# The last product of an output projection, its copy and its store in one piece instead of two, and two pairs of output rows stored by one transfer each

## The chip, the cores and the metric

The kernel runs on one core of a Trainium2 chip. The metric is the device time of one execution in microseconds (us); the number compared is the median of several executions. All times of instructions below come from one profiled execution.

## What is computed

Attention with a mask by cluster, and then a gated feed-forward layer. Each query and each key is assigned to the one of 16 centroids of its head that is nearest by angle; a query sees only the keys of its own cluster. The result, laid out as 3072 tokens of 512 features, goes through the feed-forward layer. The change touches the last matrix product alone, `@ w_out`, and the storing of its result.

```python
def _attn_ref(q, k, v, centroids):          # q, k, v: 4 x 8 x 768 x 64; centroids: 8 x 16 x 64
    ...
    mask = q_assign[:, :, :, None] == k_assign[:, :, None, :]
    scores = scale * np.matmul(q, k.transpose(0, 1, 3, 2))
    scores = np.where(mask, scores, -1000000000.0)
    ...
    return np.matmul(attn, v).astype(np.float32)

def _moe_ref(x, w_gate, w_val, w_out):      # x: 3072 x 512; w_gate, w_val: 512 x 1536; w_out: 1536 x 512
    gate = 1.0 / (1.0 + np.exp(-(x @ w_gate)))
    val = x @ w_val
    return (gate * val @ w_out).astype(np.float32)
```

## The kernel before

**Stages.** The four batches run one after another. Of each batch the 768 tokens are cut into six chunks of 128, interleaved: token 6p + c is row p of chunk c. Chunks 0, 2, 4 form the first group of a batch and chunks 1, 3, 5 the second; for the first batch the groups are cut a little differently. For each group the kernel runs attention over four pairs of heads, then `feed` (gate and value products, hidden tile hT), and then `project` for the output rows. TensorE (PE in the profile) works on attention of the next group while the feed-forward layer of the last one is interleaved with it. Only behind the last group of the last batch is there nothing to interleave.

**The output projection.** `project` (line 1292) takes two chunks at a time and forms a 2 x 2 block product (two chunks by the two halves of 256 output columns) with seven products in place of eight. Each product is six matmuls of 128 x 256 (line 1375), accumulated over the hidden features in a bank called ring. The operand sums that this needs are made by VectorE (DVE) in `add` (line 1345), into tiles named s_114, s_115 and s_116 for one pair of chunks, and into pieces of the tiles nat_64 and nat_66 for another pair that is under way at the same time. Results are put together by `halved` (line 1393 on ScalarE, ACT; line 684 where it is done on VectorE) and `summed` (line 1400), into an output tile `out2` (there are two, out20_112 and out21_113 in the program; each holds two rows of 512 columns, one per chunk). The four quarters are called c11, c12 (first chunk) and c21, c22 (second chunk); p4 is the product that ends the block, and c21 is its copy. `project` is a generator, so that for the last group of the last batch (`end`) two pairs of chunks go forward in turns: the first pair writes out_112, the last pair (`final`) writes out_113. In that group each sum of `add` is made in two halves (three hidden chunks each), and the products can begin on the first half.

**The last pair.** For the pair that ends the program, p4 is formed in two halves of 128 columns, each six matmuls of 128 x 128. The first half is copied by ACT, the second by DVE, and each half is stored by itself: the first on the queue of SyncE (SP), the second on the queue of ACT. The second row of the pair before it is also stored on ACT's queue.

**Stores.** All other rows leave by `store` (line 1431), one transfer of 128 x 512 (256 KB) per chunk, on SP's queue. A chunk whose two quarters are done early (c11, c12) is stored before the other.

**Order of the work.** Every instruction is a task. `schedule` (line 230) walks through modelled time and for each engine picks, among the tasks that could start within 0.02 us of the earliest, the one with the lowest place. The places stand in a table of numbers (PLACES), and the modelled landing time of each transfer in another (LANDINGS). Each engine then runs its tasks strictly in the order that comes out. Transfers of the SP and ACT queues take eight completion semaphores in turn, DMAHW0 to DMAHW7; a transfer waits until the eighth before it has landed. At the end of the program (line 1818, or 1822 after the change) SP waits for every one of those semaphores, in the order of their numbers, before the engines meet in a last barrier.

Of the kernel before, what the change touches and what calls it, by code (L numbers as in the profile page):

```python
# [112 lines left out]
"""  # L113

LANDINGS = """
# [12 lines left out]
"""  # L128


# [22 lines left out]
class Order:  # L153
# [76 lines left out]
    def schedule(self):  # L230
# [5 lines left out]
        for t in self.tasks:  # L236
            if not t.todo:
                wait.setdefault(t.eng, []).append(t)
        free = {e: 0.7 for e in {t.eng for t in self.tasks}}
        order, under_way, pool, twin = [], {"SP": [], "POOL": []}, (0.0, 0.0), (0.0, 0.0)  # L240
        while any(wait.values()):
            best = None
            for e, ts in wait.items():
                cand = []
                for t in ts:
                    r = t.ready
                    for tag in {b.tag for b in t.acq}:
                        f = self.free_slots(tag, sum(b.tag == tag for b in t.acq), max(t.ready, free[e]))[0]
                        r = None if f is None or r is None else max(r, f)
                    if r is not None:  # L250
                        r = max(r, free[e])
                        if t.both and r >= pool[0]:
                            r = max(r, pool[1])
                        if e == "POOL" and not t.dma and r >= twin[0]:
                            r = max(r, twin[1])
                        cand.append((r, t))
                if not cand:
                    continue
                first = min(c[0] for c in cand)
                start, t = min(  # L260
                    (c for c in cand if c[0] <= first + 0.02), key=lambda c: (c[1].due, c[0])
                )
                if best is None or start < best[0]:
                    best = (start, t)
            assert best is not None, [(t.eng, t.due, [b.tag for b in t.acq]) for ts in wait.values() for t in ts][:30]
            start, t = best
            wait[t.eng].remove(t)
            now = max(t.ready, free[t.eng])
            free[t.eng] = start + t.dur
            t.start = start  # L270
# [41 lines left out]
def kernel(  # L312
# [12 lines left out]
    B, H, S, D = q.shape  # L325
# [924 lines left out]
    HM = DM // 2  # L1250
# [41 lines left out]
    def project(b, one, two, final, many, end):  # L1292
# [144 lines left out]
        if final:  # L1437
            yield
            store(0, 0, DM, [c11, c12])
            store(1, HM, DM, [c22])  # L1440
            for lo, hi in ((0, HM // 2), (HM // 2, HM)):
                p4 = product(
                    X, False, lambda: a(1, 1), lambda i: views["t4"][:, i], [c22, weighed[-1]], [], [r1, *hs], lo=lo, hi=hi
                )
                c21 = halved(
                    lambda lo=lo, hi=hi: o2.tile[:, 1, lo:hi], lambda lo=lo, hi=hi: X()[:, lo:hi], [p4], [], [r1, o2],
                    "DVE" if lo else "ACT", hi - lo,
                )
                store(1, lo, hi, [c21], "ACT" if lo else "SP")
            h_last[h1] = h_last[h2] = p4  # L1450
            return
        if end:
# [1 line left out]
        p4 = product(X, False, lambda: a(1, 1), lambda i: views["t4"][:, i], [c22, *weighed[-NWG:]], [], [r1, *hs])  # L1454
        c21 = halved(out_part(1, 0), X, [p4], [], [r1, o2])
        h_last[h1] = h_last[h2] = p4
        store(0, 0, DM, [c11, c12])
        store(1, 0, DM, [c21, c22], "ACT" if end else "SP")

    wsums_of = {}  # L1460

# [361 lines left out]
```

## Time and profile before

| | |
|---|---|
| median of 3 runs | 309.78 us (309.48 to 310.14) |
| profiled execution, its own time | 309.38 us |
| span of that execution, first to last instruction | 307.6 us |
| PE busy | 299.2 us, 97% of the span |
| DVE, ACT busy | 249.3 us (81%), 259.0 us (84%) |
| granted TensorE clock | 1.000 of full speed |
| PE's last product ends | about 303.8 us into the span |
| last compute instruction ends (copy of the last half) | about 304.4 us |
| last store lands | about 306.4 us |

The times in the rows are counted from the start of the span. Engine PE is the matmul stream and PEld the loading of its weights, which overlaps it. A row of the timeline gives the start, the time from the first start to the last end of the instructions merged in it, engine, line and operation, and in brackets how long the engine had been idle and whom it waited for. SPq and ACTq are the queues of SP and ACT, which issue transfers. The time of the execution is 1.8 us more than the span.

### The profile page before, as it was taken

To read this page: it belongs to the slowest core of one execution; us is meant where nothing else is said; L and a number is where in the kernel's file an instruction comes from. 1 tells how busy PE (TensorE), PEld (TensorE's weight loads), DVE (VectorE), ACT (ScalarE), POOL (GpSimd) and SP (SyncE) were. 2 spreads that over 40 slices of the span, in tenths; PEclk is the share of its full clock that TensorE was granted. 3 is DMA by queue.
4 is the path that set the end of the run, shared out by engine and by line. 5 is a ranking of instruction groups with operands and counts; after the bars stand their busy time and mean duration, and the time that the engine had idled before them with its cause. 6 is when DMAs were issued, how large, how long until landed. Compare 5 with 4: busy or idle time off the path is not lost.

```text
span 307.6 us, 8905 instructions
## 1 busy us (share of the span) xinstructions
PE 299.2 (97%) x3491; PEld 237.5 (77%) x3491; DVE 249.3 (81%) x604; ACT 259.0 (84%) x449; POOL 79.2 (26%) x112
## 2 busy tenths in 40 slices
PE   7998899999999999999999999999999999999994
PEld 3676588754468688977998779987998889988974
DVE  4999996897886687889789989979778738964993
ACT  4898799884448899999999989999999998995841
POOL 5898849741022033600001301470000000000000
PEclk9999999999999999999999999999999999999999
DMA  6999999994557595931384674893210120131003
GB/s 222 368 287 181 218 202 145 181 137 85 97 90 160 111 128 166 118 47 22 84 134 90 104 119 118 178 124 29 71 37 26 40 61 34 25 74 70 0 3 136
DMA packets 97833, 34.79 MB, mean 113 GB/s; under 512 B 83152, under 2 KB 93568, under 8 KB 97792
## 3 DMA queue, kind: packets, MB, share of 16 engines
q1 hardware_dynamic: 72192, 24.57, 34.6%
q0 software_dynamic: 24880, 8.92, 29.2%
q10 hardware_dynamic: 720, 0.75, 0.7%
q8 instruction: 27, 0.44, 0.6%
q14 instruction: 14, 0.11, 0.1%
HBM read 28.87 MB, written 6.29 MB: 114 GB/s over the span
## 4 chain that ended last, share of the span: by engine, by line
PE 89%; ACT 4%; DVE 3%; DMA 2%; issue 1%; ACTq 0%; SPq 0%
PE ring L1584 25%; PE ring L1114 19%; PE ring L1375 18%; PE ring L1506 11%; PE ring L1165 10%; ACT es L1138 3%; PE ring L794 3%; DMA nat<-in_q_dram 1%; PE ring L902 1%; DVE hT L1631 1%; DMA out<-in_centroids_dram 1%; DVE t L684 1%; PE ring L942 1%; DVE even L681 0%; ACT t L909 0%
## 5 line engine op out<-in xcount | busy, mean ns | idle before, releaser
L1138 ACT ACTIVATE es<-ring,nbias 128x768 f16<-128x768 f32 (+1 forms) x189 | 169.8, 941 | 15.1 <-PE ring L1114 10.5
L1165 PEld LDWEIGHTS <-es 128*128 128x128 f16 x1152 | 51.3, 97 | 11.7 <-ACT es L1138 0.8
L1165 PE MATMUL ring<-vp,es 128*128 128x65 f16 x1152 | 56.6, 193 | 0.0
L757 POOL CAST even<-t 128x768 f16<-128x768 f32 x24 | 21.1, 892 | 116.3 <-issue 37.3
L1615 DVE TENSOR_TENSOR nat<-ring,nat 128x384 f32<-128x384 f32 x68 | 36.7, 552 | 14.9 <-ACT nat L1603 8.6
L1622 ACT ACTIVATE nat<-nat 128x384 f32<-128x384 f32 x68 | 37.3, 575 | 1.9 <-DVE nat L1615 1.9
L1584 PEld LDWEIGHTS <-wss 128*128 128x128 f16 x408 | 34.8, 98 | 2.2 <-issue 0.2
L1603 ACT COPY nat<-ring 128x384 f32<-128x384 f32 x68 | 33.9, 519 | 2.7 <-PE ring L1584 1.7
L1584 PE MATMUL ring<-nat,wv 128*128 128x192 f16 x272 | 32.6, 246 | 0.0
L1584 PE MATMUL ring<-nat,wss 128*128 128x192 f16 x272 | 32.4, 246 | 0.0
L1584 PE MATMUL ring<-x,wg 128*128 128x192 f16 x272 | 32.3, 246 | 0.2 <-DVE hT L1631 0.2
L1375 PEld LDWEIGHTS <-hT 128*128 128x128 f16 x294 | 27.2, 97 | 4.9 <-DVE hT L1631 0.4
L1375 PE MATMUL ring<-wo,hT 128*128 128x256 f16 x216 | 29.0, 272 | 0.1
L1114 PE MATMUL ring<-even 80*128 80x384 f16 (+2 forms) x120 | 26.4, 294 | 0.9 <-ACT es L1138 0.6
L1114 PE MATMUL ring<-even,odd 80*128 80x384 f16 (+2 forms) x120 | 26.8, 293 | 0.0
L1114 PE MATMUL ring<-odd 80*128 80x384 f16 x96 | 26.5, 325 | 0.1
L1114 PE MATMUL ring<-odd,even 80*128 80x384 f16 x96 | 26.4, 326 | 0.2 <-ACT es L1138 0.2
L1584 PEld LDWEIGHTS <-wv 128*128 128x128 f16 x272 | 23.3, 97 | 3.0 <-issue 0.2
L1114 PEld LDWEIGHTS <-even 80*128 80x128 f16 x216 | 19.5, 98 | 7.1 <-issue 3.5
L1114 PEld LDWEIGHTS <-odd 80*128 80x128 f16 x216 | 19.3, 98 | 6.6 <-issue 4.5
L1584 PEld LDWEIGHTS <-wg 128*128 128x128 f16 x272 | 23.1, 98 | 1.5 <-issue 0.4
L1506 PE MATMUL ring<-x,wg 128*128 128x256 f16 (+2 forms) x112 | 22.5, 326 | 0.1
(120 smaller groups left out, 519.0 us busy)
## 6 DMA issues: line engine op xcount, KB each, us to landing
out_dram<-out SPq DMA_DIRECT2D x22, 256.0 KB, 2.4
nat<-in_k_dram SPq DMA_DIRECT2D x32, 96.0 KB, 3.1
nat<-in_q_dram SPq DMA_DIRECT2D x32, 96.0 KB, 3.0
odd<-even SPq DMA_DIRECT2D x12, 192.0 KB, 3.5
vp<-in_v_dram POOLq DMA_DIRECT2D x24, 96.0 KB, 5.2
nat<-in_k_dram SPq DMA_DIRECT2D x5, 384.0 KB, 6.2
nat<-in_q_dram SPq DMA_DIRECT2D x5, 384.0 KB, 5.7
nat<-in_v_dram SPq DMA_DIRECT2D x4, 384.0 KB, 7.2
```

Of the source, the lines that this page charges most:

```text
L684: nc.vector.tensor_scalar(to, of, by, None, ALU.mult)
L757: nc.gpsimd.tensor_copy(t[:, NM[nm], cols], t32[p, nm].tile[:, cols])
L794: nc.tensor.matmul(out=ps[32 * g : 32 * g + 32, half, :QB], lhsT=cblk[:, 2 * p + half, :], rhs=t32[p, nm].tile[:, half * QB : (half + 1) * ...
L1114: nc.tensor.matmul(out=to, lhsT=kb.tile[0:80, 0, e * QB + j // 2 * 128 : e * QB + (j // 2 + 1) * 128], rhs=qb_.tile[0:80, 1, e * QB + c0 * ...
L1138: i = nc.scalar.activation(to, of, AF.Exp, bias=nbias, scale=D ** -0.5 if quarters(b, p) else scale,).ins
L1165: nc.tensor.matmul(out=av.tile[:, g : g + D + 1], lhsT=es.tile[:, i * N + c * 128 : i * N + (c + 1) * 128], rhs=vp[:, e, j, :], start=firs ...
L1375: nc.tensor.matmul(out=ps[:, lo:hi], lhsT=left_()[:, i], rhs=right(i)[:, lo:hi], start=new and i == 0, stop=i == NFC // 2 - 1, skip_group_ ...
L1506: nc.tensor.matmul(out=ps[:, :N], lhsT=ws[fc // FPG][:, dcc, fc % FPG, :], rhs=xb.tile[:, dcc, :N], start=(dcc == 0), stop=(dcc == NDC - 1),)
L1584: nc.tensor.matmul(out=ps[:, f], lhsT=w_[:, d, f], rhs=x_()[:, d], start=new and not (f or d), stop=d == 1, skip_group_check=True,)
L1603: nc.scalar.copy(held(i), bank(r_))
L1615: lambda: nc.vector.tensor_tensor(held(i), bank(r_), held(i), ALU.add), deps,
L1622: lambda: nc.scalar.activation(held(i), held(i), AF.Tanh, scale=0.5), [m], due_ffn(work), lat=0.16,
```

## The change

What was done for the pair that ends the program, in the lines of `project`:

```diff
-            for lo, hi in ((0, HM // 2), (HM // 2, HM)):
-                p4 = product(
-                    X, False, lambda: a(1, 1), lambda i: views["t4"][:, i], [c22, weighed[-1]], [], [r1, *hs], lo=lo, hi=hi
-                )
-                c21 = halved(
-                    lambda lo=lo, hi=hi: o2.tile[:, 1, lo:hi], lambda lo=lo, hi=hi: X()[:, lo:hi], [p4], [], [r1, o2],
-                    "DVE" if lo else "ACT", hi - lo,
-                )
-                store(1, lo, hi, [c21], "ACT" if lo else "SP")
+            p4 = product(X, False, lambda: a(1, 1), lambda i: views["t4"][:, i], [c22, weighed[-1]], [], [r1, *hs])
+            c21 = halved(out_part(1, 0), X, [p4], [], [r1, o2])
+            store(1, 0, HM, [c21], "ACT")
```

So p4 of that pair is one product of six matmuls of 128 x 256, copied by one instruction of ACT and stored by one transfer of 128 x 256 (128 KB) on ACT's queue. For all other pairs:

```diff
+        if b == B - 2 and chunk1 < chunk2:
+            dma(
+                "SP", lambda: out_v[b, chunk1 : chunk2 + 1 : chunk2 - chunk1].rearrange("c p m -> p c m"),
+                lambda: o2.tile, 1.34, [c11, c12, c21, c22], due_ffn(work()), uses=[o2],
+            )
+            return
         store(0, 0, DM, [c11, c12])
-        store(1, 0, DM, [c21, c22], "ACT" if end else "SP")
+        store(1, 0, DM, [c21, c22])
```

In the last but one batch (b = 2) the pairs of chunks (0, 2) and (3, 5) are stored by one transfer of 512 KB each, when all four quarters are there; the pair (4, 1), whose chunks are not in rising order, is stored by two transfers as before. The second row of the first pair of the last group moves from ACT's queue to SP's.

`schedule` now takes, on each engine, only the task with the lowest place among all that are left, so that the places alone set each engine's order:

```diff
+        line = {e: deque() for e in free}
+        for t in sorted(self.tasks, key=lambda t: t.due):
+            line[t.eng].append(t)
...
+                    if t is not line[e][0]:
+                        continue
```

The table of places is renumbered for the fewer tasks, and three entries leave the table of landings; a line of the places:

```diff
-1556 1593 1618 1616 1643 1656 1706 1735 1745 1754 1770 1777 1719 1727 1750 1783 1786 1790 1801 1828 1794 1812 1818
+1556 1593 1618 1616 1643 1656 1706 1735 1745 1754 1770 1777 1719 1727 1750 1783 1785 1788 1800 1827 1793 1811 1817
```

The banks and tiles that each instruction uses are the same as before. On PE only the last product differs. On ACT two instructions move one place each, both in the feed-forward layer of the last group: a copy of a bank (L1603) goes ahead of a tanh (L1622), and a tanh of a gate (L1673) goes ahead of another tanh (L1622).

**VectorE, the operand sums of the last group.** s_114, s_115 and s_116 are the sums of the first pair, nat_64 and nat_66 those of the last pair, out_113 is a quarter of the output. What is in brackets are the semaphores an instruction waits for. Before:

```order
L1345 TENSOR_TENSOR s_114<-hT_109 128x384 [waits DVE_49] x2
L1345 TENSOR_TENSOR s_115<-s_114,hT_108 128x384 [waits DVE_49] x2
L1345 TENSOR_TENSOR nat_64<-hT_109 128x384 x2
L1345 TENSOR_TENSOR nat_64<-nat_64,hT_109 128x384 [waits DVE_49] x2
L1345 TENSOR_TENSOR s_116<-hT_108,s_115 128x384 x2
```

And after:

```order
L1349 TENSOR_TENSOR s_114<-hT_109 128x384 [waits DVE_49] x2
L1349 TENSOR_TENSOR s_115<-s_114,hT_108 128x384 [waits DVE_49]
L1349 TENSOR_TENSOR nat_64<-hT_109 128x384 x2
L1349 TENSOR_TENSOR nat_64<-nat_64,hT_109 128x384 [waits DVE_49]
L1349 TENSOR_TENSOR s_115<-s_114,hT_108 128x384
L1349 TENSOR_TENSOR nat_64<-nat_64,hT_109 128x384 [waits DVE_49]
L1349 TENSOR_TENSOR s_116<-hT_108,s_115 128x384
L1349 TENSOR_TENSOR s_116<-hT_108,s_115 128x384 [waits DVE_49]
```

The second half of s_115 moved behind three instructions of nat_64, which each stand one place earlier.

**ScalarE and SyncE, the end of the program.** Two rows of copies and the stores that follow. The DMAHW semaphore that a store waits for is also the one it will set when it has landed; where none is shown, it is the next in turn. Before, ACT first and then SP:

```order
L1393 ACTIVATE out_112<-ring 128x256 [waits DMAHW1_49,PE_49]
L1393 ACTIVATE out_113<-ring 128x128 [waits DMAHW4_49,DVE_49,PE_49]
L441 DMA out_dram<-out_112 128x512 [waits DMAHW0_49,Activation_49]
L441 DMA out_dram<-out_113 128x128 [waits DMAHW2_49,DVE_49]
L441 DMA out_dram<-out_112 128x512 [waits DMAHW5_49,DVE_49]
L441 DMA out_dram<-out_113 128x512 [waits DMAHW6_49,DVE_49]
L441 DMA out_dram<-out_113 128x256 [waits DMAHW7_49,DVE_49]
L441 DMA out_dram<-out_113 128x128 [waits DMAHW1_49,Activation_49]
```

And after, ACT first and then SP:

```order
L1397 ACTIVATE out_112<-ring 128x256 [waits DMAHW7_49,PE_49]
L1397 ACTIVATE out_113<-ring 128x256 [waits DMAHW2_49,PE_49]
L445 DMA out_dram<-out_113 128x256 [waits Activation_49]
L445 DMA out_dram<-out_112 128x512 [waits DMAHW3_49,DVE_49]
L445 DMA out_dram<-out_113 128x512 [waits DMAHW4_49,DVE_49]
L445 DMA out_dram<-out_113 128x256 [waits DMAHW5_49,DVE_49]
L445 DMA out_dram<-out_112 128x512 [waits DMAHW6_49,Activation_49]
```

One store less is left, the second row of out_112 stands on SP instead of behind the last copy on ACT, and the last three to land set the semaphores 5, 6 and 7 where they set 0, 1 and 2.

**SyncE, the second merged store of the last but one batch.** x_107 is the input of the last group's feed-forward layer, brought in by transposing transfers. Before:

```order
L1223 DMA_TRANSPOSE x_107<-xn_102 128x3x128 [waits DMAHW6_49,DVE_49,PE_49]
L441 DMA out_dram<-out_112 128x512 [waits DMAHW7_49,DVE_49]
L1223 DMA_TRANSPOSE x_107<-xn_103 128x3x128 [waits DMAHW0_49,DVE_49,PE_49]
L441 DMA out_dram<-out_112 128x512 [waits DMAHW1_49,Activation_49]
L1223 DMA_TRANSPOSE x_107<-xn_104 128x3x128 [waits DMAHW2_49,DVE_49,PE_49]
```

And after:

```order
L1227 DMA_TRANSPOSE x_107<-xn_102 128x3x128 [waits DMAHW5_49,DVE_49,PE_49]
L1227 DMA_TRANSPOSE x_107<-xn_103 128x3x128 [waits DMAHW6_49,DVE_49,PE_49]
L445 DMA out_dram<-out_112 128x2x512 [waits DMAHW7_49,Activation_49]
L1227 DMA_TRANSPOSE x_107<-xn_104 128x3x128 [waits DMAHW0_49,DVE_49,PE_49]
```

The first of the two stores is gone, and the merged one stands where the second one stood.

More of the change, by code (lines that the diff above doesn't have):

```diff
@@ L267, in schedule @@
             wait[t.eng].remove(t)
+            line[t.eng].popleft()
             now = max(t.ready, free[t.eng])
```

74 rows, old and new, of tables (LANDINGS, PLACES) are left out of this document.

## The prediction, made before the changed kernel was run

> **What bounds the kernel now.** I read the page first: the share of each engine, then the chain of work that ended last.
>
> ```profile
> PE 299.2 (97%) x3491; PEld 237.5 (77%) x3491; DVE 249.3 (81%) x604; ACT 259.0 (84%) x449; POOL 79.2 (26%) x112
> PE 89%; ACT 4%; DVE 3%; DMA 2%; issue 1%; ACTq 0%; SPq 0%
> ```
>
> TensorE (PE) sets the time nearly everywhere. An edit elsewhere pays only where PE stands still, or behind PE's last product. So next I read the chain in order of time, for PE's last piece in it, and the timeline of what follows.
>
> ```profile
> 295.84 7.93 PE ring L1375 x75
> ...
> 302.27 1.49 PE L1375 MATMUL ring<-nat,hT 128*128 128x256 f16 x18
> 303.12 0.38 ACT L1393 ACTIVATE out<-ring 128x256 f32<-128x256 f32 x1 [2.25 <-PE ring L1375]
> 303.79 0.28 ACT L1393 ACTIVATE out<-ring 128x128 f32<-128x128 f32 x1 [0.29 <-PE ring L1375]
> 303.85 0.92 ACTq L441 DMA_DIRECT2D out_dram<-out  x2
> 304.10 0.29 DVE L684 TENSOR_SCALAR out<-ring 128x128 f32<-128x128 f32 x1 [1.23 <-ACT out L1393]
> ```
>
> The cut of the last product in two buys nothing here. ACT's copy of the first half starts at 303.79, when both halves are done (302.27 + 1.49 = 303.76), and DVE's copy of the second half waits for ACT. Product, copy, copy: all in a row. The last row's store leaves ACT's queue right after, at about 304.42 (303.85 + 0.92, less the 0.35 that one issue takes).
>
> Then come the stores, and the waits by which SP ends the program (line 1818), in three stretches of time:
>
> ```profile
> L441 ACTq DMA_DIRECT2D out_dram<-out x1: 351/351/351, 304.4 to 304.4; - x1
> out_dram<-out ACTq DMA_DIRECT2D x1, 256.0 KB, 2.1
> out_dram<-out SPq DMA_DIRECT2D x1, 128.0 KB, 1.7
> out_dram<-out SPq DMA_DIRECT2D x1, 64.0 KB, 2.0
> out_dram<-out ACTq DMA_DIRECT2D x1, 64.0 KB, 2.0
> ...
> L1818 SPq EVENT_SEMAPHORE  x3: 28/28/28, 305.9 to 306.4; - x3
> ...
> L1818 SPq EVENT_SEMAPHORE  x5: 28/28/28, 306.5 to 306.7; - x5
> L1818 SPq DRAIN  x1: 7/7/7, 306.8 to 306.8; - x1
> ```
>
> The three waits end when the last three stores land: 303.85 + 2.1, 304.09 + 2.0, 304.42 + 2.0 = 306.4. They are numbers 0, 1 and 2 of the eight completion semaphores. The five that follow are for transfers long landed, and still take about 0.06 each, one after another: 0.3 us between the last landing and the drain at 306.8. From there to the end of the span (307.6) it is a fixed 0.8.
>
> **The change, part by part.** I work from PE's last stall to the barrier, minus being a gain.
>
> *VectorE's new order.* In the last group PE goes through products of six matmuls, 0.66 apart when it doesn't wait:
>
> ```profile
> 296.83 0.82 PE L1375 MATMUL ring<-nat,s 128*128 128x256 f16 x6
> 297.24 0.62 DVE L1345 TENSOR_TENSOR nat<-hT 128x384 f16<-128x384 f16 x2
> 297.64 0.55 PEld L1375 LDWEIGHTS <-nat 128*128 128x128 f16 x6 [0.28 <-DVE nat L1345]
> 297.65 0.83 PE L1375 MATMUL ring<-nat,nat 128*128 128x256 f16 x6
> 297.78 0.62 DVE L1345 TENSOR_TENSOR nat<-nat,hT 128x384 f16<-128x384 f16 x2
> 298.31 0.62 DVE L1345 TENSOR_TENSOR s<-hT,s 128x384 f16<-128x384 f16 x2
> 298.31 0.82 PE L1375 MATMUL ring<-nat,s 128*128 128x256 f16 x6
> 298.97 0.82 PE L1375 MATMUL ring<-wo,s 128*128 128x256 f16 x6
> ```
>
> The product at 297.65 begins 0.82 after the one before it: 0.16 late, for the first sum in nat. With the second half of s_115 put behind, that sum starts one DVE step (0.27, half of 297.78 - 297.24) earlier, at 296.97, and is done by 297.32 (0.35 each), before PE is ready at 297.49. **-0.16.** What is late next? The moved half of s_115 is now done at 298.13; the fourth matmul of its product wants it at about 298.4. s_116 starts at 298.31 as before, and its first half is done at 298.66; its product would now begin at 298.81, with weights loaded a tenth ahead, at 298.70. That margin of 0.04 is the thin place. Bounds: 0 if this wait takes all back, -0.16 if nothing does. I take -0.16, since only a margin has to hold, not a new overlap.
>
> *The last product whole.* Eighteen matmuls lie in the row at 302.27: six of 256 columns, 0.11 apart, then twelve of 128. From the first start to the last it is 1.49 - 0.22 = 1.27, less 0.66 for the six, so 0.056 each for the twelve. Twelve by 0.056 is 0.67, six by 0.11 is 0.66: nothing to win or lose, **-0.01**, bounds -0.05 and +0.05. The Trainium skill (TensorE: Matmul & The Clock Gate, section Back-to-back issue gap) gives some 81 ns as the sustained spacing for 128 columns where weights change each time; by that figure the cut would cost 0.3 us more than the rows show and its end would give that back. The trace disagrees, with its 56 ns.
>
> *One copy for two.* Before: 303.79 to 304.39 (304.10 + 0.29). Now one ACT copy of 128 x 256, 0.38 by the row at 303.12: 303.79 to 304.17. **-0.22**, bounds -0.18 and -0.25 by the few hundredths between instructions.
>
> *The last store.* It was 64 KB, 304.42 to 306.4. Now it is 128 KB on the same queue. The nearest row of that size is SP's, 1.7; the nearest of that queue is ACT's store of 256 KB, 2.1. Why did 64 KB take longer than 128 KB? Three stretches of the DMA view, 304.6 to 305.3, 305.3 to 305.66 and from there to 306.0, tell which queue moved:
>
> ```profile
> q10 hardware_dynamic: 107, 0.22, 85.2%
> ...
> q1 hardware_dynamic: 124, 0.06, 62.2%
> q10 hardware_dynamic: 48, 0.05, 39.4%
> ...
> q10 hardware_dynamic: 133, 0.06, 66.6%
> ```
>
> q10 is ACT's queue, q1 SP's. The store of 256 KB, issued at 303.85, held the engines to about 305.4; the two of 64 KB stood behind it and behind each other. In the new kernel the 256 KB no longer wait behind ACT's last copy: they go out on SP when their own copy is done, at 303.12 + 0.38 = 303.50, and so move to about 305.1 (0.35 earlier). The last store is issued at 304.20 and would begin to move 0.8 later (as 303.85 did at 304.6), at 305.0. So it is held up by a tenth: 1.7 + 0.1 = 1.8 against 2.0. **-0.2**, bounds -0.3 (1.7 alone) and +0.1 (2.1, as ACT's large one).
>
> *The waits at the end.* The last store now sets semaphore 7, the last in the row, so the other seven waits are over when it lands. What stood behind the last landing, five waits of 0.06, falls away: **-0.3**. Bounds -0.3 and 0, the latter if SP's other store landed last. That one is issued 0.7 earlier (303.50 against 304.20) and takes 2.1, so it lands at 305.6 against 306.0.
>
> *The merged stores, the shorter SP queue, the two swaps on ACT.* The merged stores replace 256 KB with 512 KB at the place of the second, and their users are far away:
>
> ```profile
> 229.44 0.35 SPq L441 DMA_DIRECT2D out_dram<-out  x1
> 236.83 1.19 SPq L1223 DMA_TRANSPOSE x<-xn  x1
> ...
> 271.45 0.34 SPq L441 DMA_DIRECT2D out_dram<-out  x1
> 274.23 1.18 SPq L1223 DMA_TRANSPOSE x<-xn  x1
> x<-xn SPq DMA_TRANSPOSE x1, 2.4
> 280.81 1.46 PE L1506 MATMUL ring<-x,wg 128*128 128x384 f16 x8
> DMA to landing us min/median/max: 1.7/2.3/4.1
> ```
>
> Behind the second, at 271.45, SP's next is a transpose, issued 2.8 us later and landed at 276.6; PE reads its tile at 280.8. Another 256 KB hold the engines for some 0.8 (the 256 KB above, 304.6 to 305.4). The cover is 4.2 us. Behind the first, at 229.44, the next transpose comes 7.4 later. **0**, bounds 0 and +0.1. The two issues that go free 0.35 us of SP each, and between these rows SP waits anyway. The ACT swaps exchange neighbours:
>
> ```profile
> 285.69 0.54 ACT L1622 ACTIVATE nat<-nat 128x384 f32<-128x384 f32 x1
> 287.73 0.54 DVE L1631 SCALAR_TENSOR_TENSOR hT<-nat,ring 128x384 f16<-128x384 f32 x1
> 293.17 0.52 ACT L1622 ACTIVATE nat<-nat 128x384 f32<-128x384 f32 x1
> 294.30 0.55 DVE L1631 SCALAR_TENSOR_TENSOR hT<-nat,p 128x384 f16<-128x384 f32 x1
> ```
>
> The tanh at 285.69 goes behind a copy of 0.5; even 0.9 late it is done at 287.1, and its reader on DVE is at 287.73. The one at 293.17 is at worst a neighbour's 0.45 late, done by 294.15, and its reader is at 294.30. **0**; without that cover hT, and PE's first product of the projection, would come up to 0.4 later.
>
> *Sum.* -0.16 - 0.01 - 0.22 - 0.2 - 0.3 = -0.89, say -0.9. The span goes from 307.6 to 306.7, and the profiled execution from 309.38 to 308.5. The median of the runs shown is 309.78, 0.4 above that execution, so against it I expect **308.9**.
>
> **The rivals.** *The last store is no shorter.* It keeps ACT's 2.1: the sum is -0.16 - 0.01 - 0.22 + 0.1 - 0.3 = -0.6, **309.2**. For it: the one large store on that queue took 2.1. Against it: that store has twice the bytes, and the time goes with the bytes where nothing stands ahead (1.7 for 128 KB). The Trainium skill (DMA: Bandwidth & Descriptors, section Anatomy of one DMA, a fit for GpSimd's path) has a constant 2.0 us and the bytes by 436 GB/s on top: 2.3 for 128 KB against 2.15 for 64 KB. By it the larger store would land later and the sum would be an estimated -0.4; the row of 1.7 speaks against it.
>
> *The change takes away a chain, but not its end.* Should SP's waits cost the same wherever the last store stands among them (0.3 lost), and the stall of PE come back at s_116 (0.16 lost), -0.4 is left: **309.4**. For it is only the thin margin at 298.7; against it, the five waits without any work between them.
>
> *Slower: the merged store holds back the last group's input.* Place: the transpose at 274.23 behind the 512 KB. The slowest 256 KB store here took 4.1; were a merged one to take twice that, 8.2, and the transpose to wait for all of it, the tile would land 5.8 (8.2 - 2.4) later, at 282.4, and PE, at 280.8, would stand for 1.6. Less 0.9: +0.7, **310.5**. It decides from a delay of 4.2 on and makes the kernel slower from 5.1. Against it: the engines are held 0.8 by 256 KB, not 4.
>
> **How the numbers follow.** Forecast 0.67, first rival 0.18, second 0.10, slower 0.05. Within 0.2%, 0.62 us, this kernel's measurement can't tell a difference from none. The forecast is beyond it (-0.9, its own bounds some -0.7 to -1.0, so 308.7 to 309.1). The first rival lies at the limit, half on either side. So faster 0.67 + 0.07 = 0.74, the same 0.11 + 0.10 = 0.21, slower 0.05. The range takes in both milder rivals, 309.4 and 0.2 more since the runs before spread by 0.3 about their median, and below the sum with all bounds at their best (-1.05) and the same spread: 308.3 to 309.6.
>
> **What would show it.** In the profile of the changed kernel: no idle time of the weight load before the first nat product at about 297.5; PE's last row ending at about 303.6; one ACT copy of 0.38 behind it and an issue on ACTq right after, near 304.0; 128 KB landed in 1.7 to 1.9; the drain of SP within 0.1 of that landing, near 305.9; a span near 306.7. The forecast is wrong if the last landing is as late as 306.2, if five waits still follow it, or if PE waits anywhere before 296 where it did not.

## The result, and the profile after

| | before | changed | ratio (95% interval) |
|---|---|---|---|
| median, first comparison | 309.95 us, 22 runs | 308.88 us, 22 runs | 0.9974 (0.9961 to 0.9986) |
| median, repeated | 309.91 us, 20 runs | 308.58 us, 5 runs | 0.9953 (0.9934 to 0.9972) |
| profiled execution, its time | 309.38 us | 308.76 us | |
| its span | 307.6 us | 307.0 us | |
| start of PE's last piece in the chain of waits | 295.84 | 296.11 | |
| from there to the last landing | 10.54 | 9.93 | |
| from there to SP's drain | 10.93 | 10.02 | |

The kernel became faster. The medians differ by 1.07 us and, repeated, by 1.33 us; the intervals of the ratio are wider, from 0.4 to 1.2 us and from 0.9 to 2.0 us. The end of the program, read below, gives 0.91 us, 0.3%, which both intervals hold. The prediction was 308.9 us, and -0.89 by its sum. The ratio leaves out one slow execution of the kernel before (314.82 us) and is not the quotient of the two medians. The last two rows are differences of moments in the records of the trace, that is its single events (semaphore updates at 306.38 and 306.05 for the last landings, the drains at 306.77 and 306.13), taken before rounding; the rows quoted below round these moments to a tenth.

The page's line on the engines, of the changed kernel:

```profile
PE 299.4 (98%) x3485; PEld 237.7 (77%) x3485; DVE 249.0 (81%) x603; ACT 259.1 (84%) x449; POOL 78.9 (26%) x112
```

And the end of its chain of waits, in order of time (start, duration, what):

```profile
296.11 7.74 PE ring L1379 x69
303.85 0.02 issue
303.88 0.38 ACT out L1397
```

Nothing changed in kind. PE still sets the time, and behind it stand one copy and one store. The piece of 7.93 has become 7.74, with 69 matmuls for 75. It starts at 296.11, 0.27 later than in the profile of before: that is not in the prediction, and has an experiment of its own below. The timeline of the same stretch:

```profile
297.10 0.82 PE L1379 MATMUL ring<-nat,s 128*128 128x256 f16 x6
297.24 0.62 DVE L1349 TENSOR_TENSOR nat<-hT 128x384 f16<-128x384 f16 x2
297.65 0.64 PEld L1379 LDWEIGHTS <-nat 128*128 128x128 f16 x6
297.76 0.82 PE L1379 MATMUL ring<-nat,nat 128*128 128x256 f16 x6
...
298.41 0.82 PE L1379 MATMUL ring<-nat,s 128*128 128x256 f16 x6
298.59 0.62 DVE L1349 TENSOR_TENSOR s<-hT,s 128x384 f16<-128x384 f16 x2
...
299.07 0.82 PE L1379 MATMUL ring<-wo,s 128*128 128x256 f16 x6
...
302.37 1.47 PE L1379 MATMUL ring<-nat,hT 128*128 128x256 f16 x12
...
303.88 0.38 ACT L1397 ACTIVATE out<-ring 128x256 f32<-128x256 f32 x1 [0.27 <-PE ring L1379]
304.29 0.35 ACTq L445 DMA_DIRECT2D out_dram<-out  x1
```

Two things are to be read here. The product at 297.76 stands 0.66 behind the one at 297.10, where before the change the same two stood 0.82 apart, and the weight load ahead of it has no bracket any more: it waits for nothing. And behind PE's last row (302.37 + 1.47 = 303.84) there is one copy and one issue, where there were two copies and an issue. Then the last stores in the view of the DMA issues (count, size, median us from issue to landing):

```profile
out_dram<-out SPq DMA_DIRECT2D x3, 256.0 KB, 2.1
out_dram<-out SPq DMA_DIRECT2D x1, 128.0 KB, 1.7
out_dram<-out ACTq DMA_DIRECT2D x1, 128.0 KB, 1.8
```

And SP's waits from 305.9 on (duration in ns, first and last start in us):

```profile
L1822 SPq DRAIN  x2: 7/7/7, 306.1 to 306.2; - x2
L1822 SPq EVENT_SEMAPHORE  x1: 28/28/28, 306.1 to 306.1; - x1
```

The last store takes 1.8 (1.76 in the records) in place of 2.0. When it lands, a single wait ends, at 306.1, and the drain follows in the same tenth: the five waits that stood behind the last landing are gone. The second merged store and the transpose behind it, in the view of the DMA issues:

```profile
out_dram<-out SPq DMA_DIRECT2D x1, 512.0 KB, 3.1
...
x<-xn SPq DMA_TRANSPOSE x1, 2.3
```

And both in the timeline, with the product that reads the transposed tile:

```profile
271.71 0.39 SPq L445 DMA_DIRECT2D out_dram<-out  x1
274.50 1.18 SPq L1227 DMA_TRANSPOSE x<-xn  x1
...
281.08 1.46 PE L1510 MATMUL ring<-x,wg 128*128 128x384 f16 x8
```

The 512 KB took 3.1, and the transpose behind them 2.3, against 2.4 before. PE's product starts 0.27 later than before (281.08 against 280.81), which is the lateness that the whole execution has.

### The profile page after: what moved, and what is told of

It is laid out like the page before. It is cut to its first block, busy times and chain, and to the rows that moved or that the text cites. A ratio compares the mean times of both kernels' runs of the same rounds, so it can differ in the third digit from the quotient of the medians.

```text
span 307.0 us, 8884 instructions
## 1 busy us (share of the span) xinstructions
PE 299.4 (98%) x3485; PEld 237.7 (77%) x3485; DVE 249.0 (81%) x603; ACT 259.1 (84%) x449; POOL 78.9 (26%) x112
## 4 chain that ended last, share of the span: by engine, by line
PE 84%; DVE 7%; ACT 5%; issue 2%; DMA 1%; DVEq 0%; ACTq 0%
PE ring L1588 22%; PE ring L1118 18%; PE ring L1379 18%; PE ring L1510 11%; PE ring L1169 10%; PE ring L798 3%; ACT es L1142 3%; DVE hT L1635 1%; ACT nat L1626 1%; DVE even L685 1%; ACT nat L1607 1%; DMA out<-in_centroids_dram 1%; DVE odd L685 1%; DVE t L660 1%; PE ring L906 1%
```

## The experiments

Each kernel is the changed one but for the edit shown. All are read in the same way: from the start of PE's last piece in the chain (expectations call it the start of the hT product) to the last landing, and from there to the drain. That takes out whatever made an execution early or late before. "Turn" is the order in which transfers take the eight completion semaphores. In the edits of e1, e2, e7 and e8 the calls that only give a store its place in its engine's order are left out.

### Two stores again, and the turn alone

e1 puts the two stores of each merged pair back, and the turn moves on by two.

```diff
         if b == B - 2 and chunk1 < chunk2:
-            dma("SP", lambda: out_v[b, chunk1 : chunk2 + 1 : chunk2 - chunk1].rearrange("c p m -> p c m"), ...)
+            store(0, 0, DM, [c11, c12])
+            store(1, 0, DM, [c21, c22])
             return
```

> The changed kernel, but the two pairs of the last but one batch are stored by two transfers each again, as before the change. The turn of the completion semaphores moves on by two, so the second row of the first pair sets semaphore 0 and the last store semaphore 1. My account (the merging itself is worth nothing, its whole effect is that the last store sets semaphore 7): the tail from the start of the last group's hT product to the last landing is as in the changed kernel (296.11 to 306.05, 9.94), and behind the last landing stand six more waits of 0.06, so the drain comes 0.4 to 0.5 after the landing instead of 0.08; span and time +0.37. Rival A (the waits at the end cost the same in any order): drain 0.1 after the landing, +0. Rival B (the merged stores won or lost time themselves, by SP or by the DMA engines, between 229 and 281): products of the last group start earlier or later by more than the 0.3 that the starts of two executions differ by in the first 30 us, or PE waits for x where it did not.

e2 keeps the merged stores and moves the turn by two at the other end of the program (`od.own` holds the tasks whose place stands outside the table; while it is empty, the first pair that fits is taken).

```diff
+        if b == 0 and 2 not in (chunk1 // 2, chunk2 // 2) and not od.own:
+            for which, done in ((0, [c11, c12]), (1, [c21, c22])):
+                store(which, 0, HM, done)
+                store(which, HM, DM, done)
+            return
         store(0, 0, DM, [c11, c12])
         store(1, 0, DM, [c21, c22])
```

> The changed kernel with its merged stores; only two stores of the first batch are cut into two transfers each, far from the end, so that the turn of the semaphores moves on by two: the last store sets semaphore 1 instead of 7. My account: nothing else changes; the last landing stands where it stood (9.94 after the start of the hT product of the last group), the drain 0.4 to 0.5 behind it instead of 0.08, time +0.37. Rival A (order of the waits is free): +0, the drain 0.1 behind the landing. If e1 shows the same as this one, the merging is worth its shift of the turn and no more.

e9 takes the two stores of e1 and cuts all six stores of the first batch, so that the turn comes round to where it was.

> As e1, the pairs of the last but one batch stored by two transfers each; but all six stores of the first batch are cut into two transfers, so that the turn of the semaphores moves on by eight in all and the last store sets semaphore 7 again. My account (of the merging only the turn matters): the drain follows 0.08 behind the last landing, as in the changed kernel, and from the start of the last group's hT product to the drain it takes 10.01, within 0.03; time as the changed kernel, -0.35 against e1. Rival (two stores in place of one cost something of their own, which e1's later start hid): 10.1 or more, or a later start of the last group than any kernel with the same offset at 30 us has.

SP's waits from the last landing on, of e1:

```profile
L1828 SPq EVENT_SEMAPHORE  x7: 28/28/28, 306.2 to 306.5; - x7
L1828 SPq DRAIN  x2: 7/7/7, 306.6 to 306.6; - x2
```

The same of e2:

```profile
L1834 SPq EVENT_SEMAPHORE  x7: 28/28/28, 306.8 to 307.1; - x7
L1834 SPq DRAIN  x2: 7/7/7, 307.2 to 307.3; - x2
```

And of e9:

```profile
L1832 SPq DRAIN  x2: 7/10/13, 306.3 to 306.4; - x2
L1832 SPq EVENT_SEMAPHORE  x1: 28/28/28, 306.2 to 306.2; - x1
```

In e1 the wait that the last store ends is the first of seven, and the drain comes 0.45 behind the landing (306.59 less 306.14). In e9, with the same two stores, it is the last, and the drain comes 0.08 behind. e2, merged but turned, has seven waits from 306.8 to 307.1 and 0.45 again. Up to the last landing e1, e2 and e9 are like the changed kernel (9.93): 9.93, 9.92 and 9.94 from the start of the piece. So the whole worth of the merged stores is their count. They take two of the three transfers out of the turn that the change takes out (the third is the last store's other half), and without these two the end is 0.37 later; cutting early stores in two makes up for them as well. Rival A of e1 and e2 (the order of the waits is free) and rival B (merging wins or loses time of its own) have both fallen.

The times go the same way, but can't show the size: e1 309.38 us, ratio to before 1.0 (0.9985 to 1.0015); e2 309.16 us, 0.9988 (0.9969 to 1.0008); e9 308.89 us, 0.9965 (0.9951 to 0.9978). The end of e1 is 0.55 shorter than that of the kernel before (10.38 for 10.93), which is a little more than the interval of its ratio allows (0.46). Four of its ten executions took over 310.3 us; why is not shown.

### VectorE's order as before

The place of one task, the second half of s_115, is set back ahead of the pieces of nat_64; nothing else.

```diff
+    od.own[od.tasks[2332]] = ("entry", 2341.5)
     od.run()
```

> The changed kernel, but VectorE makes its operand sums of the last group in the order of before: the second half of s_115 ahead of nat_64. My account: the product that reads nat_64 begins 0.82 behind the one before it instead of 0.66, everything behind it moves by 0.16, and from the start of the hT product to the drain it takes 10.17 instead of 10.01; time +0.16. Rival A (the stall is only moved: in the changed kernel PE waits later, for s_116 or a bank, so the order buys nothing): 10.0, +0. Rival B (the order is what made the whole gain, by a bank or a tile that comes free earlier at the end): +0.4 or more.

PE's piece in its chain of waits:

```profile
296.35 7.91 PE ring L1387 x69
```

And in its timeline PE's two products with the weight load between them:

```profile
297.34 0.82 PE L1387 MATMUL ring<-nat,s 128*128 128x256 f16 x6
...
298.15 0.55 PEld L1387 LDWEIGHTS <-nat 128*128 128x128 f16 x6 [0.27 <-DVE nat L1357]
298.15 0.83 PE L1387 MATMUL ring<-nat,nat 128*128 128x256 f16 x6
```

The wait for nat is back (298.15 is 0.81 behind 297.34), and the piece is 7.91 against 7.74, with the same 69 matmuls: +0.17. To the drain it is 10.18, as expected (10.17). So the changed kernel had removed the stall and not moved it. Time 309.15 us, ratio 0.9984 (0.9974 to 0.9993).

### The last product and its copy in halves, one store

```diff
-            p4 = product(X, False, lambda: a(1, 1), ..., [r1, *hs])
-            c21 = halved(out_part(1, 0), X, [p4], [], [r1, o2])
-            store(1, 0, HM, [c21], "ACT")
+            for lo, hi in ((0, HM // 2), (HM // 2, HM)):
+                p4 = product(X, False, lambda: a(1, 1), ..., [r1, *hs], lo=lo, hi=hi)
+                c21 = halved(..., [p4], [], [r1, o2], "DVE" if lo else "ACT", hi - lo)
+                ...
+            store(1, 0, HM, [first_c21, c21], "ACT")
```

> The changed kernel, but the last product is again formed in two halves of 128 columns, the first copied by ScalarE and the second by VectorE, and then stored by one transfer of 128 KB on ScalarE's queue as in the changed kernel. My account: twelve matmuls of 128 columns take what six of 256 take, so PE ends within 0.05 of where it did; ScalarE's copy of the first half waits for both halves, VectorE's copy for ScalarE's, so the copies end 0.6 behind PE's end instead of 0.4; the store leaves and lands 0.22 later; time +0.2. Rival A (the halves overlap: the first copy begins when the first half is done, 0.33 ahead of PE's end): the copies end 0.3 behind PE's end, time -0.1. Rival B (small matmuls are dearer, 0.08 each in place of 0.056): PE ends 0.3 later, time +0.5.

PE's piece in its chain of waits:

```profile
296.11 7.76 PE ring L1387 x75
```

And what follows, in its timeline:

```profile
302.37 1.49 PE L1387 MATMUL ring<-nat,hT 128*128 128x256 f16 x18
...
303.89 0.28 ACT L1405 ACTIVATE out<-ring 128x128 f32<-128x128 f32 x1 [0.29 <-PE ring L1387]
304.20 0.29 DVE L696 TENSOR_SCALAR out<-ring 128x128 f32<-128x128 f32 x1 [1.23 <-ACT out L1405]
304.52 0.35 ACTq L453 DMA_DIRECT2D out_dram<-out  x1
```

This one starts its last piece at the same 296.11 as the changed kernel, so rows can be laid beside each other as they stand. The piece is 7.76 against 7.74: twelve matmuls of 128 columns cost 0.02 more than six of 256. ACT's copy starts at 303.89 against 303.88, so it does wait for both halves. DVE waits for ACT (it had been idle for 1.23, and what ended that was ACT's copy), and the store is issued at 304.52 against 304.29: +0.23. It lands 0.22 later. Rivals A (halves overlap, -0.1) and B (small matmuls dearer, +0.5) have fallen. Time 309.06 us, ratio 0.9987 (0.9970 to 1.0004).

### The same two kernels once more

> The changed kernel, unchanged, once more. In the profiled executions so far the last group's hT product started at 295.84 (before) and 296.11 (changed), and PE was 0.1 to 1.1 us later than in the profile of before from the first 30 us on, in kernels whose programs are the same there. My account: that is scatter of the start and no effect of the change; here the offset comes out anywhere in that band, while from the start of the hT product to the drain it takes 10.01 again, within 0.03. Rival (the change makes the start later): the offset is 0.27 again, within 0.1.

> The kernel before, once more. My account: its profiled execution of before was an early starter (its time 309.38 against a median of 309.8), so this one starts the last group's hT product later than 295.84, by 0.1 to 0.6, and takes 10.93 from there to the drain, within 0.03. Rival (the change makes the start later): 295.84 again, within 0.1.

The changed kernel started its last piece at 295.91 this time, 0.20 earlier than in its first profile, and took 10.01 from there to the drain. The kernel before, 312.86 us in this one execution, started it at 299.30, 3.46 later than in its own first profile, and took 10.94. So the end of each kernel repeats to 0.01 while the start of the last group moves by itself, by far more than 0.27. The rival (the change makes the start later) has fallen, but the size was missed as well: e6 was expected 0.1 to 0.6 later. Where it moved shows in PE's timeline of the first 13 us of e6, with one row of the first profile of before at the end for comparison:

```profile
9.49 0.55 PE L902 MATMUL ring<-ident,nat 128*128 128x128 f32 x3 [1.57 <-DMA nat<-in_k_dram]
10.55 2.18 PE L902 MATMUL ring<-ident,nat 128*128 128x128 f32 x9 [0.51 <-DMA nat<-in_q_dram]
...
8.43 1.20 PE L902 MATMUL ring<-ident,nat 128*128 128x128 f32 x9 [0.35 <-DMA nat<-in_q_dram]
```

And in the granted clock of that stretch (from and to, length, PE busy, PEclk, share of DMA, GB/s), again with a row of the first profile of before at the end:

```profile
8.00:10.50 2.50, 0.55 (x3) 0.99 1.04 372
10.50:14.00 3.50, 3.45 (x14) 0.52 1.06 383
...
10.50:14.00 3.50, 3.50 (x36) 1.00 1.05 384
```

PE waited 1.57 for a load of k, where it had not waited in the first profile of before, and 0.51 for one of q, where it had waited 0.35. Both loads stand at the very start of the program, where the two kernels are the same. Behind the waits PE was 2.1 later than in that first profile. Then the granted clock was 0.52 for 3.5 us: nine matmuls took 2.18, where they had taken 1.20, and PE was 3.4 later behind them. The Trainium skill (TensorE: Matmul & The Clock Gate, section What's actually happening) has the clock fall to half after an idle window of about 3.4 us. The half clock agrees; here it fell after a stretch with less idling than that: by the trace it fell at 10.45, and in the 3.4 us before, PE was busy for 1.42 in all.

### The second row on ACT's queue again

```diff
         store(0, 0, DM, [c11, c12])
-        store(1, 0, DM, [c21, c22])
+        store(1, 0, DM, [c21, c22], "ACT" if end else "SP")
```

> The changed kernel, but the second row of the first pair is stored on ScalarE's queue again, behind the last copy, as before the change. My account of the last store (it is held by the bytes ahead of it, and took less than before because these 256 KB had left earlier): the 256 KB are issued at 304.3 in place of 303.6 and move until 305.9, the last 128 KB are issued 0.38 later than in the changed kernel and move behind them, so they land 0.6 to 0.7 later (10.6 from the start of the hT product against 9.94), over 2.0 from their issue; the drain follows 0.1 after; time +0.65. Rival A (the queue doesn't matter, a 128 KB store takes 1.76): only the later issue counts, +0.38. Rival B (the wait ends with the issue, ACT's queue works both at once): +0.1 or less.

ACT and its queue in the timeline:

```profile
304.41 0.39 ACT L1405 ACTIVATE out<-ring 128x256 f32<-128x256 f32 x1 [0.28 <-PE ring L1387]
304.50 0.84 ACTq L453 DMA_DIRECT2D out_dram<-out  x2
```

The two stores in the view of the DMA issues:

```profile
out_dram<-out ACTq DMA_DIRECT2D x1, 256.0 KB, 2.1
out_dram<-out ACTq DMA_DIRECT2D x1, 128.0 KB, 2.0
```

The mechanism is the one expected: with 256 KB just ahead of it the last store takes 2.0 (2.03 in the records) in place of 1.76. That both stand on one queue is not what it takes: in the profile of before SP's 64 KB, on the other queue, took 2.0 as well, and their packets began to move at 305.4, 1.3 after their issue and when ACT's 256 KB were nearly through (the last store of the changed kernel began 0.87 after its issue). The size is not the one expected. From the start of the piece (296.65) to the last landing it took 10.27, +0.34 and not +0.65. The expectation let the 256 KB go out behind the copy, at copy + 0.4. The rows show them issued 0.09 after the copy began, at 304.50, while it ran: the issue of a transfer that waits for an earlier copy is not held by the copy on the same engine. So they are only 0.33 later than on SP, and the last store is 0.06 later and 0.27 longer. Rival A (+0.38 by a later issue alone) comes near in its sum, but has the wrong parts: the issue is not 0.38 later, and the store is not 1.76. Time 309.44 us, ratio 0.9989 (0.9959 to 1.0019).

### Less ahead of the last store

```diff
-        if b == B - 2 and chunk1 < chunk2:
+        if (b == B - 2 and chunk1 < chunk2) or (b == B - 3 and chunk1 == 0):
...
         store(0, 0, DM, [c11, c12])
+        if end:
+            store(1, HM, DM, [c22])
+            store(1, 0, HM, [c21])
+            return
         store(1, 0, DM, [c21, c22])
```

> The changed kernel with less ahead of the last store: the second row of the first pair leaves in two transfers, its half c22 as soon as that is done (about 302.4) and 128 KB of c21 at 303.6 in place of 256 KB. One pair of the second batch is merged as well, so that the number of transfers and the turn of the semaphores stay as they are. My account: the last store of the changed kernel was held by about 0.05 only, so it takes 1.70 in place of 1.76 and all ends 0.05 earlier; 9.88 from the start of the hT product to the last landing. Rival A (most of its 1.76 is waiting for the 256 KB): 1.4 or less, -0.35. Rival B (1.76 is what 128 KB cost with nothing ahead): +0.

PE's piece in its chain of waits:

```profile
296.10 7.74 PE ring L1387 x69
```

And the store issued after 304:

```profile
out_dram<-out ACTq DMA_DIRECT2D x1, 128.0 KB, 1.7
```

The last store takes 1.73 in the records, 0.03 less than in the changed kernel, and the drain comes 9.99 after the start of the piece: a gain of 0.02 to 0.03, under the 0.05 expected and far from rival A's 0.35. It is also hardly more than the scatter: in e1, e2, e3, e5 and e9, whose last stores are those of the changed kernel, the last one took 1.74 to 1.76. By the records of the packets nothing was left ahead of it in e8: SP's last data had gone at 304.97, and its own began to move at 305.13. In the changed kernel SP's last data went at 305.30, and the last store began at 305.16. So 1.73 is what these 128 KB took with nothing ahead, and in the changed kernel the last store already goes out almost unhindered; rival B (+0) can hardly be told from the account. Time 308.83 us, ratio 0.9958 (0.9942 to 0.9974), which can't be told from the changed kernel's. None of the runs is clearly better than it.

## Why the prediction was right

*What bounds the kernel.* Right: the gain came from one stall of PE and from what stands behind its last product, and the engines' busy shares did not move by more than a point. The share of PE in the chain that ended last did, from 89% to 84% (86% in the second profile of the changed kernel), but PE's products kept the same distance of 0.27 from those of before all the way from 250 us to 296.

The terms of the sum, with what took each back:

| term | predicted | measured | by |
|---|---|---|---|
| VectorE's order | -0.16 | -0.17 | e3: 7.91 to 7.74 |
| last product whole | -0.01 | -0.02 | e4: 7.76 to 7.74 |
| one copy for two | -0.22 | -0.21 | e4: issue 0.23 later, of which 0.02 is the product |
| last store | -0.2 | -0.20 | 1.96 before, 1.76 after |
| waits at the end | -0.3 | -0.30 | 0.39 before, 0.08 after; e1, e2 and e9 |
| merged stores, ACT's swaps | 0 | 0 | e1 and e9 for the stores |
| sum | -0.89 | -0.90 | 10.93 to 10.02: -0.91 |

ACT's two swaps were not tried alone. They lie at 285.7 and 293, and PE was 0.27 later than before on either side of them (281.08 against 280.81, 296.11 against 295.84), so in this profile they cost PE nothing.

*The thin place.* The prediction saw a margin of 0.04 at s_116 as what might take the stall's gain back. The product of s_116 stands 0.66 behind the one ahead of it (299.07 against 298.41), and its first half was done at 298.59 + 0.35 = 298.94. The weight load that reads it began at 298.99, 0.14 behind the load ahead of it, where the others follow by 0.11. So the load did wait, for 0.03, but the product did not. The margin held for PE, and there is nothing left of it.

*The last store.* The prediction put its 2.0 down to the 256 KB ahead, and the new one at 1.7 + 0.1. e7 puts the 256 KB back and gets 2.03; e8 clears the way and gets 1.73. So the hindrance that is left is at most 0.03 and not 0.1, which made the store 1.76 and not 1.8. The whole gain of this term comes from the second row of the first pair, which now leaves earlier on SP: with that undone (e7) the one store of 128 KB took 2.03, no less than the 1.96 of the half before. The first rival (it keeps 2.1) has fallen. The Trainium skill's fit for GpSimd's path (DMA: Bandwidth & Descriptors, section Anatomy of one DMA), by which 128 KB take an estimated 2.3, does not hold for these two queues: they needed 1.7 to 1.8.

*The waits at the end.* The second rival needed two things. That the waits cost the same wherever the last store stands fell with e1, e2 and e9; that the stall comes back at s_116 fell with e3. What decides is which semaphore the last store sets: 0, 1 or 2 leaves the others to be gone through behind it, 7 leaves none.

*Slower, by a merged store in the way.* It did not come about: the transpose behind 512 KB took 2.3.

*The step from the sum to the time.* The sum gave 306.7 for the span and 308.5 for the profiled execution; they were 307.0 and 308.76. The 0.27 between arises in the first 30 us, ahead of anything that the change touches (PE is 0.34 later there, and 0.27 from 250 us on), and e5 and e6 showed it to be scatter of the start. The forecast of the median was still right, because the difference was taken from one execution's end and put on the median of the runs. That it came as near as 0.02 (308.88 for 308.9) is luck: the median of before that it started from, 309.78 of 3 runs, became 309.95 with 22, and the medians differ by 1.07 and not by 0.89. What bears the prediction out is the sum, term by term, and not this last digit. Had the prediction been made for the profiled execution, it would have been off by a third of the gain. Of the signs it named, the moments at the end (303.6, 304.0, 305.9) all came 0.2 to 0.3 late for the same reason.

## What to carry to other kernels

Read the end of a program as a chain of its own: the last product, its copy, its store, and the waits behind the store. Cutting a last piece in two pays only if the halves really run side by side; here the timeline of the cut kernel shows product, copy and copy in a row, and the cut cost 0.2 us. Count which completion semaphore the last store sets, since here every wait that stood behind it was paid in full (0.06 each), and adding or merging transfers anywhere in the program moves it. Compare two profiles from an event late in the program, not from the start of the span.

## What was not expected of the hardware

The start of an execution moved by up to 3.5 us between runs of one kernel: 2.1 us by input loads that PE waited for, and 1.3 us more in a stretch of 3.5 us behind them at a granted clock of 0.52. That is nearly four times the gain of the whole change. Why the loads came late is not shown.

An issue on ACT's queue ran beside ACT's own copy: the first of the two transfers of e7 was issued at 304.50, while the copy ran from 304.41 to 304.80. The profile of before shows it already (issue at 303.85, copy from 303.79); the expectation of e7 had overlooked it.
